# Placing every instruction of a fused attention and expert kernel with a list scheduler

## The chip, the core and the metric

The kernel runs on one core of one Trainium2 chip. The metric is device time in microseconds of one execution; the times below are of separate executions, and one more execution was profiled.

## What is computed

Input x is 2048 tokens by 512. It is layer-normalised to xn. Part A is a 32-head attention (16 columns a head) in four segments of 512 tokens: a causal softmax inside the segment, and a running memory `M`, `z` of the segments before it, mixed by a gate. Part B scores all tokens with `w_r`, takes the best one, sends it through a gated expert of width 1792, and adds the result to that token alone. The result is x + A(xn) + B(xn).

```python
def _A_ref(x, wq, wk, wv, wo, beta):
    B, S, D = x.shape
    H = 32
    Dh = D // H
    N = 4
    L = S // N
    q = (lambda x, *d: x.transpose(*d))((x @ wq).reshape(B, S, H, Dh), 0, 2, 1, 3).reshape(B, H, N, L, Dh)
    k = (lambda x, *d: x.transpose(*d))((x @ wk).reshape(B, S, H, Dh), 0, 2, 1, 3).reshape(B, H, N, L, Dh)
    v = (lambda x, *d: x.transpose(*d))((x @ wv).reshape(B, S, H, Dh), 0, 2, 1, 3).reshape(B, H, N, L, Dh)
    phi = lambda t: jnp.where(t > 0, t + 1.0, jnp.exp(t))
    scale = Dh ** (-0.5)
    ar = jnp.arange(L)
    mask = (lambda x, dt: x.astype(dt))(ar[:, None] < ar[None, :], x.dtype) * -1000000000.0
    g = _sigmoid(beta).reshape(1, H, 1, 1)
    M = jnp.einsum('bhd,bhe->bhde', q[:, :, 0, 0, :] * 0.0, q[:, :, 0, 0, :] * 0.0)
    z = q[:, :, 0, 0, :] * 0.0
    outs = []
    for s in range(N):
        qs, ks, vs = (q[:, :, s].copy(), k[:, :, s].copy(), v[:, :, s].copy())
        logits = jnp.einsum('bhqd,bhkd->bhqk', qs, ks) * scale + mask
        p = _softmax(logits, axis=-1)
        a_dot = jnp.einsum('bhqk,bhkd->bhqd', p, vs)
        pq = phi(qs)
        num = jnp.einsum('bhld,bhde->bhle', pq, M)
        den = jnp.einsum('bhld,bhd->bhl', pq, z)[..., None] + 1e-06
        a_mem = num / den
        o = g * a_mem + (1.0 - g) * a_dot
        outs.append(o)
        pk = phi(ks)
        M = M + jnp.einsum('bhld,bhle->bhde', pk, vs)
        z = z + jnp.einsum('bhld->bhd', pk)
    o = (lambda x, *d: x.transpose(*d))(jnp.stack(outs, 2).reshape(B, H, S, Dh), 0, 2, 1, 3).reshape(B, S, D)
    return o @ wo
def _B_ref(x, w_r, w_gate, w_up, w_down):
    B, S, D = x.shape
    C = 1
    r = x @ w_r
    idx = jnp.argsort(-r, axis=-1)[:, :C]
    idx_e = jnp.repeat(idx.reshape(B, C, 1), D, axis=2)
    x_sel = jnp.take_along_axis(x, idx_e, axis=1)
    g = _silu(x_sel @ w_gate)
    u = x_sel @ w_up
    y = g * u @ w_down
    r_sel = _sigmoid(jnp.take_along_axis(r, idx, axis=1))
    y = y * r_sel.reshape(B, C, 1)
    b_off = (jnp.arange(B) * S).reshape(B, 1)
    flat_idx = (idx + b_off).reshape(B * C)
    zero = (x * 0.0).reshape(B * S, D)
    upd = _scatter_add(zero, flat_idx, y.reshape(B * C, D), axis=0)
    return x + upd.reshape(B, S, D)
x = A_x
xn = _layernorm(x, axis=-1)
return x + _A_ref(xn, A_wq, A_wk, A_wv, A_wo, A_beta) + _B_ref(xn, B_w_r, B_w_gate, B_w_up, B_w_down)
```

## The kernel before

Everything lies in SBUF in bf16; the four engines that compute are PE (matmul), ACT (exp), DVE and POOL. A token block is 128 rows, a segment four blocks. The steps:

- **Layer norm**, for each block: statistics on DVE (L143, L144), `rstd` by Ln and Exp on ACT (L147, L148), `xn` (L155) on DVE for the first segment and on POOL for the others, four PE transposes into `pT` (L160) and one copy into `xnT` (L162, L164).
- **Projections.** For head group j of segment s (8 heads, 128 columns), four matmuls each for K and Q (L206), for V by block (L249). K goes to `KT`; Q is cast to `raw_q` (L218) and scattered by eight small DMAs of SP (L210) into `QZ`, in which each head has its own 512 columns and the rows of other heads are zero. There are two QZ buffers for 16 head groups. Exponentials phi of Q and K for the memory run over ACT, POOL and DVE (L196 to L202).
- **Attention** in 160 tiles, five for each unit of four heads, two units a head group. A tile: two to four score matmuls of 1024 columns in all into `st` (L453, two buffers), one exp of 128x1024 on ACT (L458), a causal mask on POOL (L465), eight narrow PV matmuls into `acc` (L478). After five tiles DVE divides by the sums into `Oseg` (L485, L487).
- **Memory**: transposes of phi(K) (L384), products `m_ps` (L394), then for the next segments `dm` and `nm` (L411, L418), `om` on DVE (L420) and its addition on POOL (L427).
- **Expert** (`g_moe`): many matmuls of one moving column (L272, L327, L345, L364) and small DVE steps; its weights are six loads of 0.9 MB.
- **Guard** (`g_guard`): bounds the logits from the weights; a register load (L744) decides at the end on a slow path that these inputs don't take.
- **Output** for each block: transposes of `Oseg` (L505, L521), five matmuls of 512 columns with `wo` into `fin` (L511, L514; L533 to L535 and L764 in the last segment), `ob` on DVE (L497), a store by SP (L498).

All PSUM results but `st` and `acc` share two buffers (`psm`, tag "misc").

Order. PE's order is written out: the loop `for t in range(NT)` emits exp t, score t+2 and PV t-2, and `fill(t)` puts other work between tiles, by due times and a credit in PE nanoseconds (`rate`, `pick`, `step`). Ahead of the loop stand 14 warm-up matmuls (L670), the first layer norm, the first K and Q projection, two score tiles and all four V projections of segment 0. Only PE is under `manual_schedule` (L666); the orders of the other engines' queues are made by the framework from program order and dependencies. `bcl` (L169) is the step by which beta enters, for the V scale. The first loads are issued by SP (L71 to L77), the other x blocks and `wo` by ACT (L701, L702), the first three expert weights by POOL (L704), the other three by SP.

## Time and profile before

| | us |
|---|---|
| median of 3 runs | 252.86 (251.71 to 253.02) |
| the profiled execution | 253.84 |
| its span, first to last instruction | 252.0 |

Busy in the profiled span: PE 209.9 us, ACT 176.5, POOL 154.4, DVE 152.9. A timeline row gives the start, how long, engine, line, operation, written<-read, and in brackets how long the engine had been idle and what ended that; a row with x4 is four instructions merged. A row whose engine is SPq, ACTq or POOL with DMA_DIRECT2D is the issue of DMAs, not the transfer. A matmul row's length ends when its last result is written, so the next one starts before.

### The profile page before, as it was taken

The numbers are of one execution on the slowest core, as the hardware profiler recorded it, in microseconds if no ns is written. First come the engines' busy times: TensorE is split into PE (matmuls) and PEld (weight loads), VectorE is DVE, ScalarE is ACT, GpSimd is POOL, SyncE is SP. The second block draws the span as 40 slices with busy tenths as digits, with TensorE's granted clock in tenths as the row PEclk, the third lists the DMA queues.
The fourth block names the chain that finished last, engine by engine and source line by source line (L and its number), as shares of the span: only waits on it lengthen the run. The fifth ranks groups of instructions, "written<-read, shape, count | busy, mean of one in ns | idle before, by whom it ended". The sixth has DMA issues, their size and how long they took to land.

```text
span 252.0 us, 6891 instructions
## 1 busy us (share of the span) xinstructions
PE 209.9 (83%) x2717; PEld 137.3 (54%) x2717; DVE 152.9 (61%) x393; ACT 176.5 (70%) x202; POOL 154.4 (61%) x252
## 2 busy tenths in 40 slices
...
PEclk9655569999999999999999999999979999999996
...
GB/s 228 360 371 146 1 10 10 26 27 7 21 5 20 15 13 12 13 0 23 8 12 8 18 5 150 25 300 17 17 8 47 18 44 23 46 44 42 45 25 73
DMA packets 14186, 14.38 MB, mean 57 GB/s; under 512 B 3184, under 2 KB 13616, under 8 KB 14144
## 3 DMA queue, kind: packets, MB, share of 16 engines
...
q8 instruction: 23, 0.38, 0.7%
...
## 4 chain that ended last, share of the span: by engine, by line
PE 56%; DVE 15%; ACT 13%; DMA 7%; issue 3%; POOL 2%; DVEq 0%; SPq 0%; ACTq 0%
PE st L453 19%; ACT pt L458 12%; PE proj_ps L206 9%; PE acc L478 7%; PE proj_ps L249 6%; DMA beta_bc<-in_A_beta_dram 5%; PE fin L514 4%; DVE ob L497 2%; DVE raw_q L218 2%; DMA x_all<-in_A_x_dram 2%; POOL pt L465 1%; PE fin L511 1%; PE hgu_ps L345 1%; DVE KT L239 1%; DVE tp L200 1%
## 5 line engine op out<-in xcount | busy, mean ns | idle before, releaser
L458 ACT ACTIVATE pt<-st 128x1024 bf16<-128x1024 f32 x160 | 159.2, 1026 | 35.6 <-PE st L453 29.0
L465 POOL TENSOR_SCALAR_AFFINE_SELECT pt<-pt 128x512 bf16<-128x512 bf16 (+1 forms) x160 | 89.4, 563 | 78.9 <-ACT pt L458 78.5
L453 PE MATMUL st<-QZ,KT 128*128 128x256 bf16 (+3 forms) x512 | 97.2, 302 | 4.7 <-ACT pt L458 1.9
L478 PEld LDWEIGHTS <-pt 128*128 128x128 bf16 x1280 | 55.5, 96 | 25.0 <-issue 0.7
L453 PEld LDWEIGHTS <-KT 128*128 128x128 bf16 x512 | 42.1, 98 | 30.7 <-issue 10.3
L478 PE MATMUL acc<-Vaug,pt 128*128 128x17 bf16 x1280 | 55.9, 171 | 0.4 <-POOL pt L465 0.4
L206 PE MATMUL proj_ps<-xnT,wk 128*128 128x512 bf16 x64 | 20.4, 392 | 2.4 <-DVE xnT L162 1.0
L249 PE MATMUL proj_ps<-wv,xnT 128*128 128x512 bf16 x64 | 20.1, 420 | 1.3 <-DVE KT L239 0.7
L206 PE MATMUL proj_ps<-xnT,wq 128*128 128x512 bf16 x64 | 19.4, 393 | 0.5 <-DVE xnT L162 0.5
L160 PE MATMUL pT<-ident,xn 128*128 128x128 bf16 x64 | 6.7, 240 | 14.9 <-DVE xn L155 14.7
L218 DVE CAST raw_q<-proj_ps 128x512 bf16<-128x512 f32 x15 | 10.3, 689 | 14.3 <-PE proj_ps L206 12.2
L497 DVE SCALAR_TENSOR_TENSOR ob<-x_all,s,fin 128x512 bf16<-128x512 bf16 x14 | 10.4, 746 | 14.2 <-PE fin L514 14.1
L251 DVE TENSOR_TENSOR Vaug<-proj_ps,omg_bc 128x512 bf16<-128x512 f32 x16 | 11.1, 691 | 9.2 <-PE proj_ps L249 9.1
L198 POOL TENSOR_SCALAR am<-ex 128x512 bf16<-128x512 bf16 x24 | 14.9, 619 | 1.0 <-ACT ex L196 0.2
L485 DVE RECIPROCAL rr<-acc 128x16 f32<-128x16 f32 x32 | 8.1, 252 | 11.4 <-PE acc L478 11.2
L427 POOL TENSOR_TENSOR Oseg<-Oseg,om 128x512 bf16<-128x512 bf16 x11 | 12.8, 1162 | 2.0 <-DVE om L420 0.9
L487 DVE TENSOR_TENSOR Oseg<-acc,rr 128x256 bf16<-128x256 f32 x32 | 13.4, 419 | 0.6
L514 PE MATMUL fin<-wo,oT 128*128 128x512 bf16 x48 | 13.6, 377 | 0.0
L160 PEld LDWEIGHTS <-xn 128*128 128x128 bf16 x64 | 4.7, 105 | 16.1 <-DVE xn L155 15.2
L492 POOL TENSOR_SCALAR rb<-ybc,onehot,cvec 128x512 bf16<-128x512 bf16 x16 | 12.3, 768 | 1.8 <-PE fin L511 0.8
L239 DVE CAST KT<-proj_ps 128x512 bf16<-128x512 f32 x15 | 10.3, 687 | 4.9 <-PE proj_ps L206 4.7
L143 DVE BATCH_NORM_STATS2 bnst<-x_all 128x6 f32<-128x512 bf16 x16 | 10.5, 669 | 3.0 <-DMA x_all<-in_A_x_dram 3.0
...
## 6 DMA issues: line engine op xcount, KB each, us to landing
...
QZ<-raw_q SPq DMA_DIRECT2D x124, 16.0 KB, 1.8
...
```

The source lines that it names most:

```text
L198: nc.gpsimd.tensor_scalar(out=am[:], in0=ex[:], scalar1=1.0, scalar2=0.0, op0=ALU.min, op1=ALU.max)
L206: nc.tensor.matmul(ps[:], lhsT=w[:, cb, j * P:(j + 1) * P], rhs=xnT[:, cb, s * L:(s + 1) * L], start=(cb == 0), stop=(cb == NCB - 1))
L218: nc.vector.tensor_copy(out=raw[:], in_=ps[:])
L239: nc.vector.tensor_copy(out=kt[:], in_=ps[:])
L249: nc.tensor.matmul(ps[:], lhsT=xnT[:, cb, b * P:(b + 1) * P], rhs=wv[:, cb, :], start=(cb == 0), stop=(cb == NCB - 1))
L453: nc.tensor.matmul(st[:, i, off:off + n], lhsT=lh, rhs=self.qz[:, h, q0:q0 + n], start=True, stop=True)
L458: nc.scalar.activation(out=pt[:], in_=self.st.pop(k)[:], func=ACT.Exp, scale=SCALE)
L465: nc.gpsimd.affine_select(out=mv, in_=mv, pattern=pat, compare_op=ALU.is_ge, fill=0.0, base=0, channel_multiplier=-1)
L478: nc.tensor.matmul(self.acc[:, q0 // P + c, i, e, :], lhsT=pt[:, i, off + c * P:off + (c + 1) * P], rhs=Vaug[:, 4 * self.s + kb, h, :], st ...
L487: nc.vector.tensor_tensor(out=ov, in0=av[:, :, :, 0:DH], in1=rr[:, :, :, None].to_broadcast([P, 4, 4, DH]), op=ALU.mult)
L497: nc.vector.scalar_tensor_tensor(out=ob[:], in0=x_all[:, b, :], scalar=s1[:, b:b + 1], in1=fin, op0=ALU.mult, op1=ALU.add)
L514: nc.tensor.matmul(fin[:], lhsT=oT[:, cb, :], rhs=wo[:, cb, :], start=False, stop=(cb == NCB - 1))
```

## The change

`Plan` keeps a list of operations: engine, a fixed occupation in us, what is read and written, a due time `d`, an earliest time `e`. Buffers (`Buf`) are opened in rotation as the plan reaches them. `run` simulates the engines PE, ACT, DVE, POOL and SP with these durations, plus a tail for each engine between the end of an instruction and its use elsewhere (a SP transfer 1.9 unless given otherwise), and at each step emits, of the engine that can start first, the ready operation with the earliest due time. The emitted order stands on all five engines under `manual_schedule`. Nothing of the simulated times is in the program itself; there it is order and dependencies alone. The due time of tile t is 13.2 + 1.0 t us. `fill`, `rate`, `pick` and the loop over t go. All DMAs are issued by SP. The matmuls, the tile layout and the buffer counts stay. `LNAT`, `MOE_AT`, `GUARD_AT` and `FIN_AT` say at which head group layer norms, expert, guard and output blocks enter. The first head group's QZ products for heads 0 and 2 are made by DVE, 1 and 3 by ACT (before: 0 and 1, 2 and 3).

```diff
+TAIL = {"PE": 0.22, "ACT": 0.18, "DVE": 0.135, "POOL": 0.09, "SP": 1.9}
...
+class Plan:
...
+    def op(self, eng, occ, fn, r=(), w=(), d=0.0, after=(), uses=(), e=0.0, lat=None, mode=None):
+        o = dict(id=len(self.ops), eng=eng, occ=occ, fn=fn, d=d, e=e, bufs=[], mode=mode, lat=TAIL[eng] if lat is None else lat)
...
+    def run(self, dry=False, log=None):
+        free = {e: 0.0 for e in TAIL}
...
+                    t = max(t, ready[o["id"]], f, o["e"])
+                    cands.append((t, o))
+                    lo = min(lo, t)
...
+                eps = 0.03
...
+                    pick = min((o for t, o in cands if t <= lo + eps), key=lambda o: (o["d"], o["id"]))
+                t = next(t for t, o in cands if o is pick)
+                if best is None or t < best[0]:
+                    best = (t, e, pick)
...
+            end = t + o["occ"]
+            free[e] = end
+            fin = end + o["lat"]
...
+                ready[k] = max(ready[k], end if e == u["eng"] != "SP" else fin)
...
-    for b in range(4):
-        nc.sync.dma_start(out=x_all[:, b, :], in_=x_d[:, b, :])
-    nc.sync.dma_start(out=wq[:], in_=A_wq.rearrange("(cb p) n -> p cb n", p=P))
-    nc.sync.dma_start(out=wk[:], in_=A_wk.rearrange("(cb p) n -> p cb n", p=P))
-    nc.sync.dma_start(out=beta_bc[:], in_=A_beta.partition_broadcast(P))
-    nc.sync.dma_start(out=wv[:], in_=A_wv.rearrange("(cb p) n -> p cb n", p=P))
-    with nc.allow_non_contiguous_dma(reason="tiny w_r column load"):
-        nc.sync.dma_start(out=wr_col[:], in_=B_w_r.rearrange("(cb p) -> p cb", p=P))
...
-    nc.vector.memset(QZ[1][:, 0:4, :], 0.0)
-    nc.gpsimd.memset(QZ[0][:, 4:8, :], 0.0)
-    nc.gpsimd.memset(QZ[1][:, 4:8, :], 0.0)
...
+    T0, SL = 13.2, 1.0
+    def td(t):
+        return T0 + SL * t
...
+        def ps(self, shape, dtype=f32):
+            return Buf(psm, 2, shape, dtype, "misc")
...
+        def scatter(self, raw, q, dl, hs=range(8)):
+            for h in hs:
+                self.pl.op("SP", .5, lambda h=h: nc.sync.dma_start(out=QZ[q][DH * h:DH * h + DH, h, :], in_=raw[DH * h:DH * h + DH, :]), r=[raw], w=[("QZ", q, h)], d=dl[h])
+        def projq(self, n, d):
+            s, j = n // 4, n % 4
+            ps = self.proj(wq, "wq", s, j, d)
+            raw = Buf(rawp, 3, [P, L], bf16, "raw_q")
+            o = self.pl.op("DVE", .61, lambda: nc.vector.tensor_copy(out=raw[:], in_=ps[:]), r=[ps], w=[raw], d=d + 1)
+            self.misc.append(o)
+            q = n % NQ if self.gen == 0 else 0
+            self.scatter(raw, q, [td(10 * n + (5 if h >= 4 else 0)) - 3 - .5 * (3 - h % 4) for h in range(8)])
+            if s >= 1:
+                self.phi(raw, "pqT", s, j, td(10 * n) + 1)
...
+        def tile(self, s, j, w, k, q, kt, acc, d):
+            pl = self.pl
+            st = Buf(pst, 2, [P, 2, L], f32, "st")
+            pt = Buf(ptp, LAG + 4, [P, 2, L], bf16, "pt")
...
+            pl.op("PE", .435, score, r=[("QZ", q, h) for h in hs] + [kt] + ([("QZ", 1, h) for h in hs] if self.gen else []), w=[st], d=d - .9)
+            pl.op("ACT", .907, lambda: nc.scalar.activation(out=pt[:], in_=st[:], func=ACT.Exp, scale=SCALE), r=[st], w=[pt], d=d)
...
+            pl.op("POOL", .4 if k in (0, 4) else .6, mask, w=[pt], d=d + 1.1)
...
+            pl.op("PE", .2, pv, r=[pt] + [("Vaug", 4 * s + kb) for kb in range(4)], w=[acc], d=d + 2.2)
...
+            pl.op("PE", .226, mm2, r=[("pqT", s, j), ("Mbf", m, j)], uses=[pq], w=[nm], d=d + .3)
+            o = pl.op("DVE", .61, lambda: nc.vector.tensor_tensor(out=om[:], in0=nm[:], in1=rm[:, :, :, None].to_broadcast([P, 4, 8, DH]), op=ALU.mult), r=[nm, rm], w=[om], d=d + 1)
...
+                pl.op("SP", .5, go, w=[t], d=dd, e=min(dd, 16.0), lat=6.0)
+            for i, (kind, hf) in enumerate((("g", 0), ("g", 1), ("u", 0))):
+                load_mw(kind, hf, 22.0 + 4 * i)
...
+    LNAT = {1: (1, 4, 2.0), 2: (2, 14, 2.0), 3: (3, 26, 2.0)}
+    MOE_AT, GUARD_AT = 4, 9
+    FIN_AT = {}
+    for i in range(4):
+        FIN_AT[(8 + i // 2, 2 * (i % 2))] = (0, i)
+        FIN_AT[(10 + i // 2, 2 * (i % 2))] = (1, i)
+        FIN_AT[(13 + i // 2, 2 * (i % 2))] = (2, i)
...
+    def load(keys, fn, d, lat, e=0.0):
+        pl.op("SP", .5, fn, w=keys, d=d, lat=lat, e=e)
+    for b in range(4):
+        load([("x", b)], lambda b=b: nc.sync.dma_start(out=x_all[:, b, :], in_=x_d[:, b, :]), .1 * b, 2.0)
+    load(["wk"], lambda: nc.sync.dma_start(out=wk[:], in_=A_wk.rearrange("(cb p) n -> p cb n", p=P)), 1.0, 3.0)
+    load(["wq"], lambda: nc.sync.dma_start(out=wq[:], in_=A_wq.rearrange("(cb p) n -> p cb n", p=P)), 1.1, 4.0)
+    load(["beta"], lambda: nc.sync.dma_start(out=beta_bc[:], in_=A_beta.partition_broadcast(P)), 1.2, 4.0)
+    load(["wv"], lambda: nc.sync.dma_start(out=wv[:], in_=A_wv.rearrange("(cb p) n -> p cb n", p=P)), 1.3, 5.0)
+    def wr_load():
+        with nc.allow_non_contiguous_dma(reason="tiny w_r column load"):
+            nc.sync.dma_start(out=wr_col[:], in_=B_w_r.rearrange("(cb p) -> p cb", p=P))
+    for s in range(1, NSEG):
+        load([("x", 4 * s + i) for i in range(4)], lambda s=s: nc.sync.dma_start(out=x_all[:, 4 * s:4 * s + 4, :], in_=x_d[:, 4 * s:4 * s + 4, :]), 9.0 + 4 * s, 4.0, e=7.0 + 3 * s)
+    load(["wo"], lambda: nc.sync.dma_start(out=wo[:], in_=A_wo.rearrange("(cb p) n -> p cb n", p=P)), 60.0, 4.0, e=40.0)
+    load(["wr"], wr_load, 50.0, 4.0, e=18.0)
...
+    pl.op("DVE", .85, lambda: nc.vector.memset(QZ[0][:, 4:6, :], 0.0), w=[("QZ", 0, 4), ("QZ", 0, 5)], d=0)
+    pl.op("POOL", .9, lambda: nc.gpsimd.memset(QZ[0][:, 6:8, :], 0.0), w=[("QZ", 0, 6), ("QZ", 0, 7)], d=1)
+    for i in range(4):
+        pl.op("POOL", .9, lambda i=i: nc.gpsimd.memset(QZ[1][:, 2 * i:2 * i + 2, :], 0.0), w=[("QZ", 1, 2 * i), ("QZ", 1, 2 * i + 1)], d=14 + 2 * i)
+    for s in range(NSEG):
+        pl.op("POOL", .9, lambda s=s: nc.gpsimd.memset(Vaug[:, 4 * s:4 * s + 4, :, DH:DH + 1], 1.0), w=[("Vaug", 4 * s + i) for i in range(4)], d=9 if s == 0 else 20 + 2 * s)
...
+    pl.op("DVE", .1, lambda: nc.vector.tensor_scalar(out=bcl[:], in0=beta_bc[:], scalar1=-80.0, scalar2=80.0, op0=ALU.max, op1=ALU.min), r=["beta"], w=["bcl"], d=11)
+    pl.op("ACT", .2, lambda: nc.scalar.activation(out=eb[:], in_=bcl[:], func=ACT.Exp), r=["bcl"], w=["eb"], d=11)
...
+                if h in (0, 2):
+                    pl.op("DVE", .61, lambda h=h: nc.vector.tensor_scalar(out=QZ[0][:, h, :], in0=psq[:], scalar1=bdsel[:, h:h + 1], scalar2=None, op0=ALU.mult), r=[psq], w=[("QZ", 0, h)], d=9.5 + .1 * h)
+                else:
+                    pl.op("ACT", .55, lambda h=h: nc.scalar.mul(out=QZ[0][:, h, :], in_=psq[:], mul=bdsel[:, h:h + 1]), r=[psq], w=[("QZ", 0, h)], d=9.5 + .1 * h)
...
+    def values():
+        small_t["n"] = nc.values_load(small_t["nbad"][0:1, 0:1], min_val=0, max_val=1)
+    pl.op("SP", .3, values, r=["nbad"], d=td(152), e=td(120))
...
-    for s in range(1, NSEG):
-        nc.scalar.dma_start(out=x_all[:, 4 * s:4 * s + 4, :], in_=x_d[:, 4 * s:4 * s + 4, :])
-    nc.scalar.dma_start(out=wo[:], in_=A_wo.rearrange("(cb p) n -> p cb n", p=P))
-    for kind, hf in (("g", 0), ("g", 1), ("u", 0)):
-        load_mw(kind, hf, nc.gpsimd)
...
-    for t in range(NT):
-        un, k = unit_of(t)
-        un.exp(k)
-        if t + 2 < NT:
-            u2, k2 = unit_of(t + 2)
-            u2.score(k2)
-        if t >= LAG:
-            do_pv(t - LAG)
-        if t == 150:
-            nbad = nc.values_load(guard["i"][0:1, 0:1], min_val=0, max_val=1)
-        fill(t)
...
+    last = [Buf(psa, 2, [P, 2, P], f32, "acc") for i in range(2)]
...
+        if hb == 0:
+            pl.op("DVE", .3, lambda hb=hb: nc.vector.tensor_copy(out=oT3[:, 0:2, 3, :], in_=last[0][:]), r=[last[0]], w=[("oT3l", 0)], d=td(162))
+        else:
+            pl.op("ACT", .35, lambda hb=hb: nc.scalar.copy(out=oT3[:, 2:4, 3, :], in_=last[1][:]), r=[last[1]], w=[("oT3l", 1)], d=td(162))
...
+    with tc.manual_schedule(engines={ENG.PE, ENG.Activation, ENG.DVE, ENG.Pool, ENG.SP}):
+        pl.run(log=log)
```

## Rows read from the trace of the kernel before

**Rows 1.** The page: span, busy time of PE and ACT, granted clock by slices.

```profile
span 252.0 us, 6891 instructions
PE 209.9 (83%) x2717; PEld 137.3 (54%) x2717; DVE 152.9 (61%) x393; ACT 176.5 (70%) x202; POOL 154.4 (61%) x252
...
PEclk9655569999999999999999999999979999999996
```

**Rows 2.** Timeline, all engines, from 0 to 21 us.

```profile
0.81 1.82 SPq L71 DMA_DIRECT2D x_all<-in_A_x_dram  x4
0.84 2.84 ACTq L701 DMA_DIRECT2D x_all<-in_A_x_dram  x3
...
3.28 0.69 DVE L143 BATCH_NORM_STATS2 bnst<-x_all 128x6 f32<-128x512 bf16 x1 [0.58 <-DMA x_all<-in_A_x_dram]
...
5.62 1.71 POOL L125 DMA_DIRECT2D mw<-in_B_w_gate_dram  x2
...
8.01 0.30 ACT L147 ACTIVATE lnv<-MV,eps_col 128x2 f32<-128x2 f32 x1 [5.92 <-DVE MV L144]
...
18.98 0.18 DVE L169 TENSOR_SCALAR bcl<-beta_bc 128x32 f32<-128x32 bf16 x1 [9.03 <-DMA beta_bc<-in_A_beta_dram]
...
20.40 0.72 DVE L155 TENSOR_SCALAR xn<-x_all,rstd,cvec 128x512 bf16<-128x512 bf16 x2
```

**Rows 3.** DMA issues: operation, how many, KB each, median us from issue to landing.

```profile
QZ<-raw_q SPq DMA_DIRECT2D x124, 16.0 KB, 1.8
...
beta_bc<-in_A_beta_dram SPq DMA_DIRECT2D x1, 8.0 KB, 13.8
```

**Rows 4.** Windows, 2.5 to 5.0 us: busy times, clock, DMA share, GB/s.

```profile
2.50:5.00 2.50, 2.50 (x8) 0.97 (x7) 0.90 (x2) 0.00 (x0) 2.50 (x2) 1.00 0.99 343
```

**Rows 5.** Timeline, from the first projection to the fourth score tile.

```profile
23.82 1.86 PE L206 MATMUL proj_ps<-xnT,wk 128*128 128x512 bf16 x4 [0.67 <-ACT xnT L164]
...
27.43 1.41 DVE L693 TENSOR_SCALAR QZ<-proj_ps,bdsel 128x512 bf16<-128x512 f32 x2 [1.02 <-PE proj_ps L206]
...
30.30 1.94 ACT L458 ACTIVATE pt<-st 128x1024 bf16<-128x1024 f32 x2
...
30.91 5.90 PE L249 MATMUL proj_ps<-wv,xnT 128*128 128x512 bf16 x16
...
36.64 0.60 PE L453 MATMUL st<-QZ,KT 128*128 128x256 bf16 x4
```

**Rows 6.** Timeline of PE, a stretch without a wait, 61.9 to 63.4 us.

```profile
61.91 1.02 PE L206 MATMUL proj_ps<-xnT,wq 128*128 128x512 bf16 x4 [0.52 <-DVE xnT L162]
...
62.77 0.59 PE L453 MATMUL st<-QZ,KT 128*128 128x512 bf16 x2
...
63.21 0.35 PE L478 MATMUL acc<-Vaug,pt 128*128 128x17 bf16 x8
...
63.41 0.59 PE L206 MATMUL proj_ps<-xnT,wk 128*128 128x512 bf16 x2
```

**Rows 7.** The chain that ended last, in order of time: start, us, what.

```profile
117.65 0.78 PE r_ps L272 x32
```

**Rows 8.** Timeline of the end.

```profile
236.51 1.94 ACT L458 ACTIVATE pt<-st 128x1024 bf16<-128x1024 f32 x2 [0.26 <-PE st L453]
...
237.09 0.38 PE L521 MATMUL oT_ps<-ident,Oseg 128*128 128x128 bf16 x4
...
237.31 0.55 PE L478 MATMUL acc<-Vaug,pt 128*128 128x17 bf16 x16
...
243.74 0.59 PE L764 MATMUL st<-wo,oT 128*128 128x512 bf16 x2
```

**Rows 9.** Waits of PE: waiting, releaser, us in total, times, longest.

```profile
PE nm_ps L418 <- DVE raw_q L218: 1.5, 2, 0.8
```

**Rows 10.** Timeline, 36.9 us: a DVE step of 128x4 elements.

```profile
36.90 1.08 DVE L264 TENSOR_SCALAR s<-rstd 128x4 f32<-128x4 f32 x1
```

More of the change, by code (lines that the diff above doesn't have):

```diff
@@ L205, in proj_mm @@
-    def proj_mm(ps, w, s, j, cb):
-        nc.tensor.matmul(ps[:], lhsT=w[:, cb, j * P:(j + 1) * P], rhs=xnT[:, cb, s * L:(s + 1) * L], start=(cb == 0), stop=(cb == NCB - 1))
-    def scatter(raw, dst, hs=range(8)):
-        for h in hs:
-            nc.sync.dma_start(out=dst[DH * h:DH * h + DH, h, :], in_=raw[DH * h:DH * h + DH, :])
-    def g_projq(s, j, gen=0):
-        ps = ptile([P, L], f32, "proj_ps")
-        for cb in range(NCB):
-            proj_mm(ps, wq, s, j, cb)
-            yield 216
-        raw = rawp.tile([P, L], bf16, name="raw_q", tag="raw_q")
-        nc.vector.tensor_copy(out=raw[:], in_=ps[:])
-        n = 4 * s + j
-        dst = QZ[n % NQ] if gen == 0 else QZ[0]
-        free = 10 * (n - 1) - 1 if n >= NQ and gen == 0 else -1
-        now = state["t"] >= free
-        if now:
-            scatter(raw, dst)
-        if s >= 1:
-            yield ("pause", 3)
-            yield from phi_steps(raw[:], get_seg_tile("pqT", s, gen)[:, j, :])
-        if not now:
-            yield ("until", free)
-            scatter(raw, dst)
@@ L232, in g_projk @@
-    def g_projk(s, j, gen=0):
-        ps = ptile([P, L], f32, "proj_ps")
-        for cb in range(NCB):
-            proj_mm(ps, wk, s, j, cb)
-            yield 216
-        kt = ktp.tile([P, L], bf16, name="KT", tag="KT")
-        kt_tiles[(s, j, gen)] = kt
-        nc.vector.tensor_copy(out=kt[:], in_=ps[:])
-        if gen:
-            scatter(kt, QZ[1])
-        if s <= NSEG - 2:
-            yield ("pause", 3)
-            yield from phi_steps(kt[:], get_seg_tile("pkT", s, gen)[:, j, :])
@@ L661, in run_all @@
-    def run_all(gen):
-        for _ in gen:
-            pass
-    manual = tc.manual_schedule(engines={ENG.PE})
-    manual.__enter__()
-    warm_ps = pst.tile([P, 2, L], f32, name="st", tag="st")
-    for i in range(14):
-        nc.tensor.matmul(warm_ps[:, i % 2, :], lhsT=zero_t[:, 0:P], rhs=zero_t[:], start=True, stop=True)
-    ln_stats(0, 2)
-    ln_rstd(0, 2)
-    ln_stats(2, 4)
-    ln_xn(0, nc.vector)
-    ln_xn(1, nc.vector)
-    ln_rstd(2, 4)
-    ln_T(0)
-    ln_xn(2, nc.vector)
-    ln_T(1, nc.scalar)
```

1090 lines of the change are left out of this document (583 added, 507 removed).

## Prediction

> **What bounds the kernel now.** I read the page first [rows 1]: PE is busy 83% of 252.0 us, ACT 70%, DVE and POOL 61% each, and the granted clock is low in slices 2 to 6. So there are two regimes: a start in which nobody works, and a long middle in which PE looks full.
>
> The start, by its timeline [rows 2]: SP issues the first four blocks of x at 0.81, and at once ACT issues 1.5 MB of later x and POOL, from 5.62, the first expert weights. The first block of x is being counted at 3.28, but beta, issued at 5.14, lands 13.8 us later [rows 3], while the DMA engines move 343 GB/s [rows 4]: it stands in a crowd, not in a slow load. DVE has `bcl` (L169), which wants beta, ahead of the statistics, idles 9.03 us before it, and the first xn comes at 20.40 [rows 2]. From there one chain runs: first projection 23.82, QZ 27.43, first exp 30.30. PE then does all 16 V matmuls at half clock, and the fourth score tile starts only at 36.64 [rows 5].
>
> The middle. PE's busy share counts the drain of each matmul, so I use the distance from start to start where PE didn't wait [rows 6]: four projection matmuls 0.86 (61.91 to 62.77), one score tile 0.44, one PV tile of eight 0.20. One-column matmuls come every 0.024 (0.78 for 32) [rows 7], four transposes take 0.22 (237.09 to 237.31) [rows 8]. What PE must issue, at the full clock:
> 160 tiles x (0.44 + 0.20) = 102.4; 48 projections x 0.86 = 41.3; 16 output blocks x 5 x 0.215 = 17.2; 45 fours of transposes x 0.22 = 9.9; memory products, 24 fours like transposes = 5.2; 344 narrow matmuls x 0.024 = 8.3; guard 8 x 0.215 and the rest 1.9. Sum 186.2 us.
> Before 36.64 PE has done 4 x 0.22 of transposes, 8 x 0.215, two score tiles and 16 x 0.215, 6.9 in all. The other 179.3 take from 36.64 to 244.17 (243.74 plus two matmuls [rows 8]), 207.5 us. So 28.2 us, 13.6% of the middle, are gaps, and after the last matmul 7.8 us remain to 252.0 (output sums, stores, the end). PE's gaps are many and short: a typical row is two waits, 1.5 us together, for a DVE cast ahead of a memory product [rows 9].
>
> A rule speaks against PE as the bound: the Trainium skill (Perfetto Trace Analysis, Identifying the Most-Contended Engine) says matmul busy share is no good measure and weight-load busy share is. By that PE has 54% [rows 1] and ACT with 70% would be the bound. I keep the start-to-start sum, which needs neither share; the other reading is the third rival.
>
> **The change part by part.** The arithmetic, the tiles and the buffer counts stay; 186.2 us of PE issue is neither added to nor taken from.
>
> Loads. The x loads and `wo` leave ACT's queue and the expert weights leave POOL's; all go through SP in planned order. x (0.5 MB), wk, wq, beta, wv and one later x block come first, then the scatter of `raw0`, which waits for the first projection, and only behind it the other x blocks and the expert weights. SP pays some 0.46 us an issue (1.82 for four [rows 2]); seven more are 3.2 us, on a queue with idle time. With SP's ring alone, x blocks follow at 0.13 MB / 343 GB/s = 0.4 us: the fourth by 4.5 instead of after 7. wk then ends near 6, wq 7.5, beta 8, wv 9.5, all ahead of need. Beta's wait goes: if the plan puts `bcl` early all the same, it costs at most up to 8, some 2 us. What is late next is the statistics themselves.
>
> Start chain: first block 3.28 as now [rows 2], two statistics 1.4, then aggregate, Ln, Exp and cvec at up to 0.30 each (the Ln row of 8.01 [rows 2]) 1.2: first xn at 5.9 instead of 20.40, 14.5 earlier. The same chain behind it, [rows 5]: projection 23.82 to 9.3; and as DVE now makes both heads (0, 2) that the first tile reads, the score needs the two products of 1.41 from 27.43, so 28.9 becomes 14.4. If the clock holds through the start, 8 x 0.215 = 1.7 is saved: 12.7. I take 14.4, since the clock sank in slice 2 [rows 1] and the transposes of the new start are thin as well. In the wait for QZ one V block (0.9) fits: PE has then done 0.9 + 1.7 + 0.9 = 3.5 of its work. The other 12 V matmuls now go between scores by due time instead of ahead of the fourth tile.
>
> Middle. 186.2 - 3.5 = 182.7 remains, so without a single gap PE ends at 14.4 + 182.7 = 197.1, the span at 204.9. Gaps: between 0 (the stretch of [rows 6] has none inside) and the present rate, 182.7 x 28.2 / 179.3 = 28.7. I take 12.5, a little under half. For that: the plan issues a PE step only when its operands are modelled ready, with a tail per engine, so gaps like [rows 9] go where other work exists, and it does, the two score and two misc PSUM buffers permitting. Against zero: the engines stay in order, so any step that runs longer than its fixed cost stops all behind it; and the same DVE and POOL work is pressed into fewer microseconds. Such a step is in the trace: `s` (L264) took 1.08 us [rows 10] for 128x4 elements while POOL worked on bf16 blocks. The plan knows it as 0.1. The Trainium skill (SBUF — State Buffer, SBUF: two separate sides) says DVE and GpSimd take their common port as an exclusive lock and the loser blocks; this row is consistent with it, and by it the gaps would move to the upper end, 28.7.
>
> Small edits. Memsets are split and move between DVE and POOL: POOL covers them, it has no mask to do before the first exp; without that cover they cost their length, about 1. Splitting the last `acc` in two and giving ACT one copy touches the final 7.8, which I keep whole: between 0 and 1 gained. The guard's register load now stands mid-stream: counted at nothing, under 1. SP waits in order: a scatter waiting for `raw` or for QZ to come free holds back later scatters, expert loads and stores; whoever reads QZ waits. Its price is the fourth rival; here nothing, since a scatter lands in 1.8 [rows 3] and the plan reckons 1.9.
>
> Sum: 14.4 + 182.7 + 12.5 + 7.8 = 217.4 us of span. The profiled execution took 253.84 for its 252.0, 1.8 more, and the median of the runs, 252.86, lies 1.0 under that: 217.4 + 1.8 - 1.0 = 218.2, say **218**.
>
> **Rivals.**
> First, the order leaks as before: frozen durations don't hold, and the gaps stay at 28.7. 14.4 + 182.7 + 28.7 + 7.8 = 233.6, time 234. For it: [rows 9, 10]. Against: the gaps now sit at operands that a planner can see.
> Second, a nearly dense PE: gaps up to 5, and the clock held: 12.7 + 182.7 + 0 to 5 + 7.8 = 203 to 208, time 204 to 209. For it: stretches like [rows 6]. Against: 28.2 us lost in a kernel that already had a due-time order on PE.
> Third, ACT is the bound. Two exps in a row end 1.94 after the first starts, one takes 1.02, so one each 0.92 [rows 8]; 160 x 0.92 = 147, and the rest of ACT 176.5 - 160 x 1.02 = 13 [rows 1]. From a first exp at 15 to a last at 175, and 13.5 from the last exp's end (238.45) to the end of the span: 189, time 190. Against: PE's issue alone ends the span at 204.9.
> Fourth, slower: SP as the bound. All 124 scatters, the stores and all loads stand in one ordered queue planned with a landing of 1.9. 15 head groups follow the first; the forecast has 252.9 - 218 = 35 us to lose, 2.3 per group. If scatters land not 1.8 but over 4.2 us after issue, group after group, because expert loads of 0.9 MB are ahead or a store holds the queue, PE stops at the first score of each, and the kernel is slower than before: at 5 us, 15 x 3.1 = 47, time 265. Against: only six expert loads exist, 0.9 MB / 343 GB/s = 2.6 us each.
> Fifth, that it doesn't do what it says: not-before times of loads are only planned, nothing in the program waits for them. What precedes `raw0`'s scatter on SP really holds back; a block of x may come early, which costs 1.5 us of transfer behind the weights. Inside the range.
>
> **How the numbers follow.** Forecast, gaps 7 to 20, time 212 to 226: 0.52. Leaking order, 226 to 236: 0.20. Dense: 0.20. ACT as the bound: 0.02. Something between 236 and 251: 0.02. SP as the bound: 0.04, of which 0.01 falls within 0.5%, about what a measurement of this kernel can tell from no change. So faster 0.96, same 0.01, slower 0.03. For 8 in 10 the range takes the forecast, most of the dense case and the leaking one up to its price: 207 to 234.
>
> **What would show it.** Right: `bcl` without a long wait and first xn near 6; first exp near 15; no gap between the second and the tenth exp like that from 30 to 36; PE starts at a pace that leaves some 7% of gaps; PE's last matmul near 209; 8 us behind it. Wrong: a late first exp (loads still crowd), PE waiting for QZ or for scatters of SP (fourth rival), `st` waiting for ACT in most tiles (third), DVE steps far above the plan's fixed costs with PE waiting for misc PSUM (first).

## The result: faster, but 13.5 us later than predicted

The changed kernel takes 231.5 us (median of 4 runs, 229.41 to 232.1), the kernel before 252.92 beside it (4 runs, 251.71 to 253.02): a ratio of 0.915, 95% interval 0.908 to 0.921. That is 21.4 us gained where 34.9 were forecast. The time lies outside the forecast's own interval (212 to 226). The range holds it only because it was drawn out to the price of the first rival (234), and what made it so late is something else than that rival's leak.

The page of the changed kernel: span and instructions, PE's busy time, then granted clock and DMA share in 40 slices.

```profile
span 230.0 us, 6827 instructions
...
PE 204.0 (89%) x2680; PEld 133.5 (58%) x2717; DVE 158.2 (69%) x392; ACT 172.3 (75%) x203; POOL 151.7 (66%) x252
...
PEclk9769999999999988988999999999999999999965
DMA  5800597031000012660000010010100001110020
```

Against [rows 1], PE is busy 89% instead of 83%, the low clock of five slices at the start has shrunk to two, and new dips stand in slices 15, 16, 18 and 19 (81 to 109 us).

Timeline of its start, all engines (start, us, what; in brackets the idle time before it and what ended it).

```profile
3.23 3.93 POOL L772 MEMSET QZ<- 128x1024 bf16 x4
...
6.21 3.80 DVE L321 TENSOR_SCALAR xn<-x_all,rstd,cvec 128x512 bf16<-128x512 bf16 x2
7.10 1.72 POOL L774 MEMSET Vaug<- 128x128 bf16 x3
8.47 2.43 POOL L574 TENSOR_TENSOR sq<-wq 128x512 bf16<-128x512 bf16 x2
...
9.92 0.99 DVE L315 SCALAR_TENSOR_TENSOR cvec<-MV,rstd 128x2 f32<-128x2 f32 x1
...
12.71 0.17 DVE L789 TENSOR_SCALAR bcl<-beta_bc 128x32 f32<-128x32 bf16 x1
...
13.44 1.86 PE L358 MATMUL misc<-xnT,wk 128*128 128x512 bf16 x4 [0.67 <-ACT xnT L336]
...
16.58 0.75 DVE L811 TENSOR_SCALAR QZ<-misc,bdsel 128x512 bf16<-128x512 f32 x1 [0.22 <-PE misc L358]
...
17.43 0.69 ACT L813 ACTIVATE QZ<-misc,bdsel 128x512 bf16<-128x512 f32 x1 [0.74 <-POOL am L367]
18.15 0.75 DVE L811 TENSOR_SCALAR QZ<-misc,bdsel 128x512 bf16<-128x512 f32 x1 [0.82 <-ACT QZ L813]
18.94 0.69 ACT L813 ACTIVATE QZ<-misc,bdsel 128x512 bf16<-128x512 f32 x1 [0.82 <-DVE QZ L811]
18.95 0.81 PE L436 MATMUL st<-QZ,KT 128*128 128x512 bf16 x5 [1.20 <-DVE QZ L811]
...
19.52 1.01 ACT L439 ACTIVATE pt<-st 128x1024 bf16<-128x1024 f32 x1
```

The crowd of loads is gone: `bcl` has no wait where it idled 9.03 us [rows 2], and the first xn is ready to start at 6.21 instead of 20.40. But the two xn together take 3.80 us where they took 0.72 [rows 2]. POOL's memsets and squares lie beside them: the first xn takes 2.75 and ends 0.14 behind POOL's last memset (8.82), the second 1.11 and ends 0.15 behind the first square (9.85). Even a step of 128x2 elements, beside the second square, takes 0.99. The first projection comes at 13.44 (9.3 was forecast), at half clock. Then the four QZ products go DVE, ACT, DVE, ACT, each ahead of the next, and the first exp is at 19.52 (30.30 before [rows 5]).

Windows of the middle, with each engine's busy time (instructions), then granted clock, DMA share and GB/s.

```profile
82.00:84.20 2.20, 2.20 (x69) 2.11 (x66) 0.75 (x5) 1.58 (x3) 2.20 (x4) 1.00 0.09 22
84.20:87.60 3.40, 3.18 (x19) 1.53 (x18) 2.00 (x5) 1.77 (x2) 1.10 (x2) 0.50 0.08 19
88.00:99.00 11.00, 10.89 (x226) 8.22 (x226) 5.96 (x16) 10.34 (x13) 7.70 (x13) 1.00 0.55 175
101.30:104.70 3.40, 3.18 (x25) 2.05 (x23) 2.04 (x6) 1.91 (x2) 1.14 (x3) 0.50 0.35 118
```

Twice PE runs 3.4 us at half clock (1.2 GHz). Ahead of the first stretch it was busy without a break, with 64 of the expert's one-column matmuls among its work (L680, 81.0 to 83.2). Ahead of the second stand 112 of them (L695, 88.0 to 99.2) and then a wait, which ends 0.57 us before the clock falls:

```profile
100.69 0.38 PE L436 MATMUL st<-QZ,KT 128*128 128x512 bf16 x1 [0.87 <-DMA QZ<-raw_q]
```

The five scatters that SP issued at 94.2 to 97.3, right behind an expert load of 0.9 MB (93.64), took 3.9 to 6.3 us to land, where the median is 1.8.

Timeline of its end, and the last row of the kernel before.

```profile
213.16 0.81 PE L861 MATMUL misc<-wo,oT 128*128 128x512 bf16 x3
...
215.54 0.59 PE L436 MATMUL st<-QZ,KT 128*128 128x512 bf16 x2
...
216.23 1.02 ACT L439 ACTIVATE pt<-st 128x1024 bf16<-128x1024 f32 x1 [2.43 <-PE st L436]
...
217.78 0.37 PE L457 MATMUL acc<-Vaug,pt 128*128 128x17 bf16 x8 [1.06 <-POOL pt L448]
...
220.32 0.65 PE L875 MATMUL st<-wo,oT 128*128 128x512 bf16 x2
...
221.63 1.40 DVE L878 SCALAR_TENSOR_TENSOR ob<-x_all,s,st 128x512 bf16<-128x512 bf16 x2
```

```profile
245.05 1.40 DVE L497 SCALAR_TENSOR_TENSOR ob<-x_all,s,st 128x512 bf16<-128x512 bf16 x2
```

Twelve output matmuls of the last blocks (L859, L861) stand ahead of the last score, so ACT idles 2.43 us before the last exp, and PE waits for its mask. The last `ob` ends at 223.03, 2.06 behind PE's last matmul (2.1 before), and the span ends 6.95 later (5.58 before).

In the terms of the forecast: the start is 18.95 instead of 14.4 (+4.55). PE's last matmul ends at 220.97, so its gaps are 220.97 - 18.95 - 182.7 = 19.3 instead of 12.5 (+6.8). What follows takes 9.0 instead of 7.8 (+1.2). Together 12.6, the whole miss of the span (230.0 for 217.4).

### The profile page after: what moved, and what is told of

Same layout as the page of the kernel before. It is cut to its first block, busy times and chain, and to the rows that moved or that the text cites. A ratio compares the mean times of both kernels' runs of the same rounds, so it can differ in the third digit from the quotient of the medians.

```text
span 230.0 us, 6827 instructions
## 1 busy us (share of the span) xinstructions
PE 204.0 (89%) x2680; PEld 133.5 (58%) x2717; DVE 158.2 (69%) x392; ACT 172.3 (75%) x203; POOL 151.7 (66%) x252
## 4 chain that ended last, share of the span: by engine, by line
PE 55%; DVE 20%; ACT 7%; issue 5%; DMA 5%; POOL 4%; SPq 1%; POOLq 0%; ACTq 0%
PE st L436 19%; PE misc L358 9%; PE acc L457 8%; ACT pt L439 6%; PE misc L552 4%; PE misc L400 4%; DVE bnst L305 3%; DMA x_all<-in_A_x_dram 3%; POOL pt L448 2%; DMA QZ<-raw_q 2%; DVE KT L390 2%; DVE Oseg L423 1%; PE misc L550 1%; DVE ob L532 1%; PE misc L331 1%
## 5 line engine op out<-in xcount | busy, mean ns | idle before, releaser
L436 PE MATMUL st<-QZ,KT 128*128 128x512 bf16 (+3 forms) x507 | 95.8, 302 | 3.3 <-DVE QZ L811 1.2
L358 PE MATMUL misc<-xnT,wk 128*128 128x512 bf16 x57 | 18.4, 406 | 1.2 <-ACT xnT L336 0.7
L358 PE MATMUL misc<-xnT,wq 128*128 128x512 bf16 x55 | 17.3, 395 | 0.5 <-issue 0.2
L400 PE MATMUL misc<-wv,xnT 128*128 128x512 bf16 x58 | 16.6, 378 | 1.0 <-DVE raw_q L815 0.6
L532 DVE SCALAR_TENSOR_TENSOR ob<-x_all,s,misc 128x512 bf16<-128x512 bf16 x12 | 9.0, 747 | 9.2 <-PE misc L552 9.0
L402 DVE TENSOR_TENSOR Vaug<-misc,omg_bc 128x512 bf16<-128x512 f32 x16 | 11.0, 689 | 4.6 <-PE misc L400 4.3
L423 DVE TENSOR_TENSOR Oseg<-acc,rr 128x256 bf16<-128x256 f32 x32 | 13.5, 423 | 0.9
L379 DVE CAST raw_q<-misc 128x512 bf16<-128x512 f32 x15 | 10.3, 688 | 5.5 <-PE misc L358 3.0
L390 DVE CAST KT<-misc 128x512 bf16<-128x512 f32 x15 | 10.3, 687 | 3.5 <-PE misc L358 2.8
L552 PE MATMUL misc<-wo,oT 128*128 128x512 bf16 x40 | 10.7, 378 | 0.4
L331 PE MATMUL misc<-ident,xn 128*128 128x128 bf16 x64 | 6.8, 240 | 4.3 <-DVE xn L321 2.9
```

The lines of the kernel that those rows point to most:

```text
L358: self.pl.op("PE", .216, lambda cb=cb: nc.tensor.matmul(ps[:], lhsT=w[:, cb, j * P:(j + 1) * P], rhs=xnT[:, cb, s * L:(s + 1) * L], start= ...
L390: o = self.pl.op("DVE", .61, lambda: nc.vector.tensor_copy(out=kt[:], in_=ps[:]), r=[ps], w=[kt], d=d + 1)
L400: self.pl.op("PE", .216, lambda cb=cb: nc.tensor.matmul(ps[:], lhsT=xnT[:, cb, b * P:(b + 1) * P], rhs=wv[:, cb, :], start=(cb == 0), stop ...
L423: pl.op("DVE", .345, lambda: nc.vector.tensor_tensor(out=Oseg[s][:, j, :, 4 * w:4 * w + 4, :], in0=av()[:, :, :, 0:DH], in1=rr[:, :, :, No ...
L436: nc.tensor.matmul(st[:, i, off:off + n], lhsT=lh, rhs=QZ[q][:, h, q0:q0 + n], start=True, stop=True)
L552: pl.op("PE", .216, lambda cb=cb: nc.tensor.matmul(fin[:], lhsT=oT[:, cb, :], rhs=wo[:, cb, :], start=False, stop=(cb == NCB - 1)), r=[oT, ...
```

## The experiments

Theory: the order holds on the chip, and the miss is made of three places. Two of them the plan can't see, POOL beside DVE in the start and the clock in the middle; the third it makes itself, the output matmuls ahead of the last score. Rival: the plan's fixed durations fail everywhere, and every part of the middle slips. Ratios are to the kernel before on the same chip.

**The changed kernel again (e0), for comparison.**

> The changed kernel once more, as the measure for the runs beside it. Both theories: 229 to 232.5 us, first exp about 19.5. Whether the granted clock falls to .5 between 80 and 105 us again is open: if it is a matter of the program's order in that stretch it falls in the same place, if it is the chip's own state it may not.

230.24 us, ratio 0.911 (0.907 to 0.915), first exp 19.60. The clock is half at 84.4 to 87.8 and 101.4 to 104.8, the same places on another chip: the program sets the place. Whether the clock falls there is not set by the program alone, as far as the executions tell: of e0's six, two took 232.5 us at a mean granted clock of 0.949 (the profiled one is of these), the other four 229.6 to 230.3 at 0.963 to 0.971.

**Loads alone and order alone.** e3 keeps the new order and puts the loads back on their old queues; e4 keeps the old order and puts the loads on SP.

```diff
 # e3, on the changed kernel
-load(["wo"], lambda: nc.sync.dma_start(out=wo[:], ...), 60.0, 4.0, e=40.0)
+nc.scalar.dma_start(out=x_all[:, 4 * s:4 * s + 4, :], ...)    # s = 1, 2, 3; wo too
+nc.gpsimd.dma_start(out=early[(kind, hf)][:], ...)             # first three expert weights
 # e4, on the kernel before
-    nc.scalar.dma_start(out=x_all[:, 4 * s:4 * s + 4, :], ...)
-    load_mw(kind, hf, nc.gpsimd)
+    nc.sync.dma_start(out=x_all[:, 4 * s:4 * s + 4, :], ...)   # s = 1 behind wr_col; wo too
+    load_mw(kind, hf, nc.sync)
```

> The changed kernel in its own order, but the later x blocks and wo are issued by ACT and the first three expert weights by POOL at the start, as in the kernel before. Theory (the crowd of loads delays wk, wq, beta and wv to 14 to 22 us after issue): first projection at about 17, V matmuls not before 22, first exp near 23, time 4 to 6 us longer, 235.5 to 237.5; less than the 14 us that the start was late before, since bcl no longer stands ahead of the statistics. Rival (the order alone made the start): first exp within 1 us of 19.5, time 231 to 232.

> The kernel before with the loads alone changed: x of segment 1 issued by SP behind wv, the other x blocks, wo and the first three expert weights by SP behind the scatter of the first raw_q; SP's order is as written. Theory (most of the start is the crowd of loads, the middle is the order): first xn near 8, first exp 12 to 14 us earlier than 30.3, time 239 to 242, so that loads give more than half of the 21.4 us. Rival (the frozen order gives the gain in all stages): 247 to 252.

e3: 237.28 us, ratio 0.935 (0.926 to 0.944), as expected. The start waits for the crowd again, with the first exp at 27.59, later than the 23 expected:

```profile
18.06 1.89 PE L367 MATMUL misc<-xnT,wk 128*128 128x512 bf16 x4 [4.23 <-DMA wk<-in_A_wk_dram]
...
21.19 0.92 DVE L802 TENSOR_SCALAR bcl<-beta_bc 128x32 f32<-128x32 bf16 x1 [7.44 <-DMA beta_bc<-in_A_beta_dram]
```

e4: 246.37 us, ratio 0.973 (0.966 to 0.979); 239 to 242 was expected, so missed. Its fourth score tile starts at 23.13 instead of 36.64 [rows 5], 13.5 earlier, but only 7.6 us arrive at the end (253.92, the kernel before beside it, less 246.37). Timeline of SP, then PE, where the rest goes:

```profile
24.76 1.24 SPq L126 DMA_DIRECT2D mw<-in_B_w_gate_dram  x2
26.05 1.28 SPq L126 DMA_DIRECT2D mw<-in_B_w_up_dram  x1
27.43 18.93 SPq L211 DMA_DIRECT2D QZ<-raw_q  x18
...
38.96 1.03 PE L454 MATMUL st<-QZ,KT 128*128 128x512 bf16 x2 [6.26 <-DMA QZ<-raw_q]
```

The scatter stands behind 2.7 MB of expert weights on the same queue: its landing takes up to 11.5 us where the median is 1.8, PE waits 6.26, and the clock is half from 37.1 to 43.9. This is the fourth rival's mechanism, in an order that lets it happen. e11 tests it: the same kernel, the three expert loads behind the third group's scatter.

```diff
-    for kind, hf in (("g", 0), ("g", 1), ("u", 0)):
-        load_mw(kind, hf, nc.sync)
...
+        if t == 12:
+            for kind, hf in (("g", 0), ("g", 1), ("u", 0)):
+                load_mw(kind, hf, nc.sync)
```

> The kernel before with the loads on SyncE's queue as in e4, but the three expert loads issued behind the third query group's scatter (twelve score tiles later). Theory (e4 gave its gain back to the scatter that queued behind 2.7 MB of expert loads): no wait of 6 us on raw_q's scatter at 39 us, no half clock at 37 to 44, 237 to 241 us against 246.4. Rival (the old order gives the gain back by itself, at the next tiles that wait): the waits go elsewhere and the time stays at 244 to 247.

240.44 us, ratio 0.951 (0.944 to 0.958). The wait is gone, and 37 to 44 us run at full clock:

```profile
26.98 10.79 SPq L211 DMA_DIRECT2D QZ<-raw_q  x16
37.82 1.12 SPq L126 DMA_DIRECT2D mw<-in_B_w_gate_dram  x2
```

Later scatters still land in up to 10.0 us, but PE doesn't wait for them (DVE does once, 1.4). So of the changed kernel's 21 us, 12.6 (253.0, the kernel before beside it, less 240.44) are to be had by moving loads alone, if they also stand behind the scatters. The changed kernel moves the loads too, but spreads them between the scatters; these land in up to 6.3 us, and PE waits for one once, 0.87.

**POOL off DVE's first xn (e1).**

```diff
-    pl.op("POOL", .9, ... QZ[1] ..., d=14 + 2 * i)
+    pl.op("POOL", .9, ... QZ[1] ..., d=14 + 2 * i, e=0.0 if i < 2 else 13.0 + i)
-    pl.op("POOL", .9, ... Vaug ..., d=9 if s == 0 else 20 + 2 * s)
+    pl.op("POOL", .9, ... Vaug ..., d=9 if s == 0 else 20 + 2 * s, e=0.0 if s == 0 else 20.0 + 2 * s)
-    pl.op("POOL", 1.0, ... sq ..., d=dd)
+    pl.op("POOL", 1.0, ... sq ..., d=dd, e=30.0)
```

> The changed kernel with POOL kept quiet while DVE makes the first four xn: two of the four QZ1 memsets, the Vaug memsets of segments 1 to 3 and the guard's squares get an earliest time behind the first masks, so POOL meets them after an instruction that waits for ACT. Theory (POOL holds up DVE's xn at the common port): first xn from 3.80 for two to about 0.75, first projection from 13.4 to about 9.7, first exp from 19.5 to about 16, and as PE is the bound the end moves with it: 231.5 to 227.5 or 228.5. Rival one (the loads in flight make xn slow): xn stays near 3.8, time unchanged. Rival two (given back: the late QZ1 memsets or masks hold up the second head group): the first exp is early, but the 16th exp is not, time within 1 us.

223.34 us, ratio 0.883 (0.876 to 0.889): 3 points better than the changed kernel, more than the 3 to 4 us expected.

```profile
6.10 0.70 DVE L321 TENSOR_SCALAR xn<-x_all,rstd,cvec 128x512 bf16<-128x512 bf16 x2
...
9.32 1.02 PE L358 MATMUL misc<-xnT,wk 128*128 128x512 bf16 x4 [0.67 <-ACT xnT L336]
...
13.41 0.75 DVE L811 TENSOR_SCALAR QZ<-misc,bdsel 128x512 bf16<-128x512 f32 x1 [0.82 <-ACT QZ L813]
...
14.21 0.81 PE L436 MATMUL st<-QZ,KT 128*128 128x512 bf16 x5 [1.19 <-DVE QZ L811]
```

The two xn take 0.70 again, the first projection is at 9.32 and at full clock, the score at 14.21. The forecast's figures are 9.3 and 14.4. Up to the projection its chain was right and its cover was not. That the score agrees too is luck, two errors that cancel: at full clock the step from the projection to the first QZ product is 2.53 instead of 3.61 [rows 5], and DVE's two products, in turns with ACT's, take 2.31 instead of 1.41; for a full clock the forecast had 12.7. The granted clock is full up to 211.5 us: in this execution it doesn't fall beside the expert part either (3.4 us of the gain, by the plan's table below), and the end behind the last `ob` is 1.6 shorter (5.3). These two are the gain beyond the start.

**QZ from SBUF (e8, with e1).** In e1 the QZ products still take turns, although the two engines have nothing to do with each other's results. They read one PSUM tile.

```diff
+    pl.op("DVE", .61, lambda: nc.vector.tensor_copy(out=raw0[:], in_=psq[:]), r=[psq], w=[raw0], d=9.4)
-    ... tensor_scalar(out=QZ[0][:, h, :], in0=psq[:], ...), r=[psq], ...
+    ... tensor_scalar(out=QZ[0][:, h, :], in0=raw0[:], ...), r=[raw0], ...
-    ... nc.scalar.mul(out=QZ[0][:, h, :], in_=psq[:], ...), r=[psq], ...
+    ... nc.scalar.mul(out=QZ[0][:, h, :], in_=raw0[:], ...), r=[raw0], ...
```

> The run with POOL's early memsets put off (e1), and beside it the first tile's four QZ products read from the raw_q copy in SBUF instead of the projection in PSUM, so that DVE and ACT need not take turns. Theory (the turn-taking delayed the first exp): QZ on DVE and on ACT run side by side right behind raw_q; first exp at about 13.6 instead of 14.78, scatter issued about 2 us earlier, 222 to 223 us (about 1 under the 223.3 of e1). Rival (the first score waits for something else): first exp stays at 14.6 or later and the time at 223.3.

221.54 us, ratio 0.880 (0.874 to 0.885). Its timeline has DVE and ACT side by side and the first exp at 13.44, 1.34 earlier than in e1:

```profile
11.42 0.68 DVE L810 CAST raw_q<-misc 128x512 bf16<-128x512 f32 x1
...
12.14 0.81 DVE L813 TENSOR_SCALAR QZ<-raw_q,bdsel 128x512 bf16<-128x512 bf16 x2
...
12.20 1.33 ACT L815 ACTIVATE QZ<-raw_q,bdsel 128x512 bf16<-128x512 bf16 x2 [0.36 <-DVE raw_q L810]
...
13.44 4.75 ACT L439 ACTIVATE pt<-st 128x1024 bf16<-128x1024 f32 x5
```

The first exp is what the theory said; in total time e8 and e1, measured on different chips, overlap.

**Output matmuls behind the last score (e2).**

```diff
-    ... after=busy, d=td(158))
+    ... after=busy, d=td(161.3))
-    ... r=[("oT3", cb), "wo"], w=[key], uses=[t], d=td(158))
+    ... r=[("oT3", cb), "wo"], w=[key], uses=[t], d=td(161.3))
```

> The changed kernel with the first four matmuls of each of the last four output blocks due behind the last PV (161.3 instead of 158 in tile time), so that the last score tiles go ahead of them and they fill the waits for the last exp and mask. Theory (due times put 3.4 us of PE work ahead of the last score, and PE then waits 2.7 us with nothing left): the gap of 1.06 ahead of the last PV and most of the 2.43 of ACT go, time 2 us shorter, 229.5. Rival (the last DVE steps and stores are the end anyway): within 0.5 us.

226.71 us, ratio 0.894 (0.886 to 0.902), 4 to 5 below the changed kernel, where 2 were expected. The profiles part it: by exp 144 it is 0.5 us ahead (it has one stretch at half clock, not two), by PE's last matmul 2.6, so the end's order gives 2.1; and the last `ob` to the end of the span takes 5.5 instead of 6.95, which the edit doesn't touch. That last piece is the next run's.

**The end without the slow path (e7).**

```diff
-    if not opts.get("no_slow"):
+    if opts.get("slow"):
         with tc.If(nbad > 0):
             slow_path()
```

> The changed kernel with the slow path behind the branch left out of the program (it is never taken on these inputs; the guard and its register load stay). Theory (the end is long because SyncE fetches instructions behind the branch after the last store): the time from the last ob on DVE to the end of the span falls from about 7 us to 3 to 5, 226 to 229 us in all. Rival (the end is the landing of the stores): end as long as before, 229 to 232.

224.66 us, ratio 0.889 (0.885 to 0.893), 5.6 below e0 on the same chip. Its page and its end:

```profile
span 223.1 us, 6847 instructions
...
q14 instruction: 11, 0.09, 0.1%
...
219.08 1.40 DVE L878 SCALAR_TENSOR_TENSOR ob<-x_all,s,st 128x512 bf16<-128x512 bf16 x2
```

From the last `ob` to the end are 2.7 us, where the changed kernel has 6.95, e0 7.4, the kernel before 5.6. The stores land inside these 2.7, so the rest was not theirs. In the trace of the changed kernel SP's last steps stand at 226.08 and 228.13, each behind a packet of the instruction queue (20 packets on q14 there, 11 here): by these times SP fetches program on the far side of the branch. The other microsecond of the 5.6 may go with a half-clock stretch: this profile has one (83.8), not two.

**The clock in the middle (e9).** The expert part due one tile later.

```diff
-    MOE_AT, GUARD_AT = 4, 9
+    MOE_AT, GUARD_AT = 5, 9
```

> The changed kernel with the expert part due one tile (10 us) later; its one-column matmuls then come about 9 to 12 us later. Theory (the two stretches at half clock between 84 and 105 us belong to these one-column matmuls): no half clock between 82 and 90 us; if it falls again, at 93 to 98 and 110 to 116. Rival (the clock falls there whatever PE does): again at 84.2 and 101.3. The time is that of the changed kernel, 228 to 232.5, under 228 if the clock does not fall at all.

232.79 us, ratio 0.923 (0.918 to 0.928), just above the 228 to 232.5 expected. Windows, and PE's row ahead of the fall:

```profile
84.00:90.00 6.00, 5.64 (x71) 3.41 (x67) 4.39 (x15) 5.73 (x8) 3.88 (x7) 1.00 0.02 4
91.90:98.70 6.80, 6.80 (x96) 4.66 (x93) 1.95 (x5) 3.69 (x5) 2.02 (x5) 0.50 0.08 19
99.00:112.00 13.00, 13.00 (x221) 8.83 (x218) 7.92 (x21) 11.02 (x14) 8.14 (x15) 1.00 0.48 152
```

```profile
91.33 0.54 PE L680 MATMUL misc<-onehot,x_all 128*128 128x1 bf16 x16 [0.88 <-DVE onehot L667]
```

The half clock moved along, a little less than expected: 6.8 us from 91.9, 0.6 behind the first of the 64 matmuls of L680 (91.3 to 95.3), and nothing at 84 or 101. L695, now spread over 15 us and with no wait behind it, is not followed by a fall. So the clock doesn't fall there whatever PE does, and the stretch goes with the expert part. That it is the one-column matmuls is not shown: here PE had also waited 0.88 us just before.

The other profiles don't separate it. The second stretch stands in the changed kernel, e0, e2, e3, e6 and e10, each time within 0.7 us behind a wait of 0.7 to 1.3 us for a scatter. It is missing in e7 and e8, which have no such wait, but also in e1 (0.62) and e12 (0.90). The first stretch (changed kernel, e0, e6, e7) has no wait ahead of it, and e1, e2, e3, e8, e10 and e12 issue the same 64 matmuls as closely and stay at full clock there. What decides it is open.

**The register load later (e10).**

```diff
-    pl.op("SP", .3, values, r=["nbad"], d=td(152), e=td(120))
+    pl.op("SP", .3, values, r=["nbad"], d=td(152), e=td(143))
```

> The changed kernel with the guard's register load put about 3.8 us later in the program, behind the moment at which its input is ready. Theory (PE's 1.0 us wait on nbad_i is the cost of the load's place): the wait before PE's load is gone, PE stands still for 0.5 us at most, 0.5 to 1 us less in all: 229 to 230. Rival (the load itself holds PE): the gap of 1 us stays.

PE's wait on `nbad_i` (1.0 us in the changed kernel) is gone, and between exps 96 and 120 the kernel slips 2.2 us against its plan instead of 3.2. In total 230.56 us (229 to 230 expected), ratio 0.909 (0.901 to 0.917): no difference from the changed kernel that can be told.

**All together (e6: e1, e2 and e8; e12: e10 as well).**

> All three mends together: POOL's memsets put off (e1), QZ from raw_q (e8), the last segment's output matmuls due behind the last score (e2). If the parts add up by the sum of the changed kernel's late start (-5), the QZ turns (-1) and the end (-2): 219 to 222 us. If they don't add, because the time is set by the clock in the middle: 223 to 227.

> POOL's memsets put off, QZ from raw_q, output matmuls behind the last score, and the register load later (e1, e8, e2 and e10 in one). The 217.9 us of the three together less 0.5 to 1: 216.5 to 218. If the register load's wait is paid back at the next tile: 217.9.

e6: 217.93 us, ratio 0.861 (0.855 to 0.866). e12: 216.47 us, ratio 0.857 (0.853 to 0.862), the best version: 36 us below the kernel before, and some 14 below the changed one. Its page:

```profile
span 214.2 us, 6862 instructions
...
PE 200.5 (94%) x2717; PEld 131.6 (61%) x2717; DVE 153.1 (71%) x392; ACT 171.2 (80%) x203; POOL 150.6 (70%) x252
...
PEclk9999999999999999999999999999999999999996
```

e6 came out just under its expectation (219 to 222): the parts add, as far as the clock lets one tell. Its profiled execution took 219.2 us at a mean granted clock of 0.973, the other three 216.4 to 218.5 at 0.985 to 0.989.

**Plan against chip.** The scheduler keeps a list of the starts it planned. Exps of the trace minus exps of the plan, in us (exp number across):

```
        0     16    56    64    72    96    120   159
after   7.0   7.9   9.5   11.2  14.1  14.5  17.7  18.2
e10     7.5   8.4   10.0  10.2  13.2  13.7  15.9  16.6
e7      6.8   7.7   9.1   10.9  11.6  12.2  14.9  15.4
e1      2.3   4.4   5.6   5.8   6.8   7.4   10.1  10.8
e6      0.8   1.7   2.5   4.2   6.9   7.4   10.1  10.6
e12     1.1   1.9   2.6   2.9   4.2   4.7   6.4   7.2
e8      0.9   1.7   2.5   2.8   3.0   3.8   6.5   7.0
```

A failing plan would lose steadily. This one loses at places: 7.0 before the first exp, 4.6 between 56 and 72 (the two half-clock stretches and the wait between them; e8, with neither, loses 0.5 there), 3.2 between 96 and 120 (1.0 of it the register load). e6 and e8 share their plan up to the end and part by 3.9 us at just those 16 exps, where e6 has two stretches of 3.4 us at half clock and a wait of 0.72.

The column of exp 64 parts them. The first stretch costs about 1.4 (56 to 64: 1.7 or 1.8 with it, 0.2 or 0.3 without). From 64 to 72 the wait and the second stretch together cost 2.7 to 3.0, e12's wait of 0.90 without a stretch 1.3, e8 with neither 0.2. So about 3 of the 4 us are the clock's and about 1 the wait's.

## Why the prediction was right and wrong

**Right: where the bound was, and the first gain.** The crowd of loads was the start's cause (e3 brings it back: first exp at 27.59 for 19.52, and 6 us slower than the changed kernel, 237.28 for 231.5). The start chain up to the projection is what was written, once POOL is out of the way (e1); behind it two errors cancel. PE's start-to-start sum as the floor held: in e12 PE's gaps are 206.85 - 13.16 - 182.7 = 11.0, in e8 208.98 - 13.02 - 182.7 = 13.3, on both sides of the 12.5 taken, though in mended orders. ACT's share rose to 80% in e12 without becoming the bound, so the third rival's 190 was not near. By the Trainium skill's rule that the text weighed (Perfetto Trace Analysis, Identifying the Most-Contended Engine: for PE, weight-load busy share and not matmul busy share) e12 would have PE at 61% and ACT as the bound; the rows disagree: by the start-to-start sum 182.7 of PE's 193.7 us are issue.

**Wrong: the start, +4.55.** The step that failed is the sentence on small edits, that "POOL covers" the memsets and that they cost about 1 without that cover. POOL was indeed idle. The cost was DVE's: the first xn takes 2.75 instead of 0.35 beside POOL's memsets, the second 1.11 beside a square, and the chain came 4.1 later (13.44 for 9.3). The row that shows this mechanism was in the text [rows 10], and was used for the middle alone, where it decided nothing. The Trainium skill (SBUF — State Buffer, SBUF: two separate sides) states an exclusive lock between DVE and GpSimd, the loser blocked for a whole instruction; the stretched steps agree with it in kind, each ending close behind a POOL instruction, though the first xn waited for four in a row. By these rows the memsets cost most, 2.4 us; e3, whose squares come only at 21.0, still has 2.89 for its two xn. The remaining 0.4 is the QZ turn less what the clock gave back. The sum put DVE's two products in a row (1.41 as in [rows 5]), but ACT's product stands between them, 16.58 to 18.90, 0.9 more; the clock, full again from 15.9, saves 0.5 ahead of them. The Trainium skill (PSUM — Partial Sum Buffer, PSUM bank collisions raise a hardware error) says that a program must keep two engines from one bank at a time, reads too; the program does so here, and e8, which reads SBUF, runs both at once.

**Wrong: the gaps, +6.8.** 12.5 was a fair figure for the order but held nothing for the clock after the start, which only the dense rival named, as something that holds, and it put the wait for scatters at nothing. The two stretches and the wait for a scatter between them cost about 4 (4.6 against 0.5 in 16 exps), about 3 of it the clock's. The end's order costs 2.1 (e2): the plan gives the output matmuls a due time of 171.2 and the last score 171.3, which reading the due times would have shown. The register load, "nothing, under 1", is 1.0. These are 7.1 for 6.8.

**Nearly right: the end.** 9.0 for 7.8: the way from PE's last matmul to the last `ob` is as before, and what grew is the stretch behind it, 5.58 to 6.95. That this stretch is 2.9 and 4.3 us longer than without the slow path (2.7, e7) was not seen; the 7.8 was kept as one piece.

**The rivals.** The first was right on the time (234 for 231.5) and wrong on the reason: gaps of 28.7 were not seen, and the losses sit in places. The fourth is real as a mechanism (e4: landing 11.5, wait 6.26), but in the changed kernel, where scatters behind expert loads land in up to 6.3, PE's longest wait for one is 0.87. The fifth is true and harmless: the second segment of x, planned for 10.0, is issued at 4.72; the loads behind the first scatter are held by it.
